# Keys and first queries of batch 0 turned by TensorE instead of DMA, and a first batch cut into more, smaller chunks

## The chip, the cores and the metric

The kernel runs on one core of a Trainium2 chip. The metric is the time of one execution on the device in microseconds (us). A core has TensorE (PE, with PEld for its weight loads), VectorE (DVE), ScalarE (ACT), GpSimd (POOL) and SyncE (SP), which in this kernel issues transfers; 16 DMA engines move data.

## The reference

Attention in which a query sees only keys of its own hash bucket, followed by a gated feed-forward layer. In short, with 4 batches, 8 heads, 768 tokens, a head size of 64 and 6 hash bits:

```python
q_bits = (np.einsum('bhsd,dk->bhsk', q, proj) > 0)          # keys alike; 6 bits make a bucket
mask   = q_bucket[:, :, :, None] == k_bucket[:, :, None, :]
scores = np.where(mask, scale * np.matmul(q, k.transpose(0, 1, 3, 2)), -1e9)
attn   = softmax(scores)                                    # over the keys
x      = np.matmul(attn, v)   -> (3072 tokens, 512)
out    = (x @ w_a) * (x @ w_b) @ w_out                      # 512 -> 1536 -> 512, all in float32
```

## The kernel before

Tokens are worked through in chunks. `BLOCKS` gives the length of each chunk in units of 128 tokens; the three later batches have three chunks of 256, batch 0 has chunks of 128, 128, 256 and 256. For each chunk the kernel does the attention of all 8 heads (units of one head and 128 queries) and then the feed-forward layer, `moe`. Chunks 0 and 1 (`N32`) do the layer in float32, while the weights' fp16 halves are not there yet; all later chunks use fp16 products, each float32 operand in a high and a low half.

**Keys and queries** go through `split` (L684), four pairs of heads of keys for a batch (`kprep`), queries once or twice per chunk (`qprep`). Its steps in batch 0: a bf16 product of the raw rows with themselves on PE (`gram`, L650) gives a bound, DVE reduces it (L637), and a power of two follows (`power_of`, L588 to L603); the high fp16 half is scaled (L621 on ACT, L623 on DVE), the low half is the rest (L717, DVE). High and low half, side by side in `kt0` or `qt0`, are turned (tokens from partitions to columns) by a transposing DMA that SP issues (L724) into half 1 of the buffer `trk` or `trq`. From that, PE makes the hash bits' products (L736, `kb` and `qb`), ACT copies the negated part (L754), DVE makes bits (L757) and penalty columns (L763, L766), which go beside a copy of the high half (L614) in `hp`; a second transposing DMA (L773) turns that into half 0. Only then can PE make scores (L1167).

**A unit**: scores, their maximum (`mx`, L1187, DVE), scale and bias (L1195, L1199), exponential (L1208, ACT). The exponentials are turned too: those of chunk 0 (`NTURN`) by PE in float32 (L1143, copies L614), the others by DMA after a split into fp16 halves. Then PE makes the weighted values `av` (L1221, L1236). When a chunk's units are done, `x` is scaled, turned, and the layer's products follow: first layer L1394 (float32) or L1402 (fp16), the gate `g` (L1431, DVE, with ACT's part L1423), second layer L1467.

**Weights** come as 128x1024 pieces (L886, issued by SP), and three operations make proper float32 out of each: two on ACT (L897, sometimes POOL at L899, and L907) and a join on DVE (L915). Six bf16 products (L933) bound them; later fp16 halves are made (L623, L858).

**The order** is not that of the code. Every operation goes through `op(engines, cost, run, key, r=..., w=...)`; `Plan.issue` starts them in a planned time, each engine in its own order, by the priorities of a table `PLACES` and on the engines that a table `ENGINES` names, where an operation allows several. On the chip each engine then runs its instructions in that fixed order and waits on semaphores for what an instruction needs. SP's queue of transfers is such an order too: a transfer that waits for its source holds up what stands behind it.

The step that the change replaces, in `split`, is this one, and a second of its kind for half 0:

```python
op(
    "SP", T_ISSUE,
    lambda: nc.sync.dma_start_transpose(out=dst.t[:, 1], in_=fl(pt[0])),
    key, r=[(pt[0], "hi"), (pt[0], "lo")], w=[(dst, 1)], svc=0.175 * n, hold=[dst],
)
```

Of the kernel before, what the change touches and what calls it, by code (L numbers as in the profile page):

```python
# [1568 lines left out]
```

## Time and profile before

| what | value |
|---|---|
| three timed runs | 914.08, 918.28, 919.96 us (median 918.28) |
| the profiled execution's own time | 915.97 us |
| its span (first to last instruction) | 914.2 us |
| PE busy | 867.5 us, 95% |
| DVE busy | 621.5 us, 68% |
| ACT busy | 569.5 us, 62% |
| POOL busy | 434.8 us, 48% |
| transfers of SP's queue | 147.44 MB, 82.9% of 16 DMA engines' span |

How to read what follows. A row of the table by stage has the stretch in us from the span's start, its length, then for PE, PEld, DVE, ACT and POOL the busy us and in brackets the number of instructions, then the granted clock of PE (1.00 is full speed), the DMA engines' busy share and GB/s. A row of the timeline has the start, the length, engine, line, operation, output<-inputs with shapes, the count, and in square brackets the idle time ahead of it and what ended it. A row of the lines has line, engine, operation, output<-inputs, shape and count, then busy us and mean ns of one, then idle time ahead of it and what ended it.

### The profile page before, as it was taken

To read this page: it belongs to the slowest core of one execution; us is meant where nothing else is said; L and a number is where in the kernel's file an instruction comes from. 1 tells how busy PE (TensorE), PEld (TensorE's weight loads), DVE (VectorE), ACT (ScalarE), POOL (GpSimd) and SP (SyncE) were. 2 spreads that over 40 slices of the span, in tenths; PEclk is the share of its full clock that TensorE was granted. 3 is DMA by queue.
4 is the path that set the end of the run, shared out by engine and by line. 5 is a ranking of instruction groups with operands and counts; after the bars stand their busy time and mean duration, and the time that the engine had idled before them with its cause. 6 is when DMAs were issued, how large, how long until landed. Compare 5 with 4: busy or idle time off the path is not lost. (4 is left out here: it accounts for less than half of the span.)

```text
span 914.2 us, 23474 instructions
## 1 busy us (share of the span) xinstructions
PE 867.5 (95%) x9361; PEld 662.7 (72%) x9361; DVE 621.5 (68%) x1441; ACT 569.5 (62%) x1126; POOL 434.8 (48%) x359
## 2 busy tenths in 40 slices
...
GB/s 303 253 323 290 274 123 123 160 145 180 193 191 195 158 157 140 136 182 200 199 185 115 158 158 143 161 192 158 196 186 124 118 162 118 131 121 105 36 1 24
DMA packets 444062, 148.94 MB, mean 163 GB/s; under 512 B 416688, under 2 KB 436272, under 8 KB 443952
## 3 DMA queue, kind: packets, MB, share of 16 engines
q1 hardware_dynamic: 443952, 147.44, 82.9%
q8 instruction: 73, 1.20, 0.5%
...
## 5 line engine op out<-in xcount | busy, mean ns | idle before, releaser
L617 POOL TENSOR_TENSOR a<-e,a 128x768 f16<-128x768 f32 x184 | 311.3, 1694 | 218.2 <-DVE a L614 90.1
L1402 PE MATMUL ab<-xT,wz 128*128 128x256 f16 x3168 | 374.5, 273 | 7.1 <-DVE g L1431 7.1
L1402 PEld LDWEIGHTS <-wz 128*128 128x128 f16 x3168 | 303.5, 98 | 55.8 <-issue 9.1
L1208 ACT ACTIVATE e<-s,bias,sc 128x768 f32<-128x768 f32 x192 | 189.5, 987 | 123.3 <-DVE bias L1199 116.0
L1187 DVE TENSOR_REDUCE mx<-s 128x1 f32<-128x768 f32 x192 | 182.4, 952 | 70.5 <-PE s L1167 69.7
L1467 PE MATMUL o<-wz,g 128*128 128x512 f16 (+1 forms) x840 | 216.2, 392 | 1.8 <-DVE g L1431 1.8
L1447 POOL TENSOR_TENSOR g<-g,g 128x256 f16<-128x256 f32 x132 | 92.2, 698 | 156.4 <-ACT g L1442 156.0
L1167 PE MATMUL s<-trk,trq 76*128 76x384 f16 (+1 forms) x768 | 155.3, 329 | 9.6 <-DMA trk<-hp 4.9
L1431 DVE SCALAR_TENSOR_TENSOR g<-ab,ab,a 128x256 f32<-128x256 f32 x132 | 63.5, 481 | 113.9 <-ACT a L1423 97.1
L1236 PEld LDWEIGHTS <-at 128*128 128x128 f16 x3312 | 117.1, 98 | 21.0 <-issue 3.5
L1467 PEld LDWEIGHTS <-g 128*128 128x128 f16 x792 | 75.0, 98 | 68.9 <-issue 0.6
L1236 PE MATMUL av<-vh,at 128*128 128x64 f16 x2208 | 121.0, 193 | 0.7 <-DMA at<-a 0.7
L1423 ACT ACTIVATE a<-ab,ab 128x256 f32<-128x256 f32 x132 | 62.2, 471 | 92.0 <-PE ab L1402 87.2
L1167 PEld LDWEIGHTS <-trq 76*128 76x128 f16 (+1 forms) x768 | 71.6, 99 | 56.5 <-issue 16.0
L614 ACT CAST a<-e 128x768 f16<-128x768 f32 x109 | 90.4, 829 | 1.8 <-DMA at<-a 0.2
L1442 ACT CAST g<-g 128x256 f16<-128x256 f32 x132 | 52.9, 401 | 41.2 <-DVE g L1431 39.3
L1236 PE MATMUL av<-vl,at 128*128 128x64 f16 x1104 | 62.5, 194 | 0.0
L614 DVE CAST a<-e 128x768 f16<-128x768 f32 x70 | 42.8, 614 | 21.4 <-ACT e L1208 20.9
L1394 PE MATMUL ab<-xT,wz 128*128 128x128 f32 x384 | 49.0, 279 | 1.6 <-DVE g L1431 1.6
L1394 PEld LDWEIGHTS ab<-xT,wz 128*128 128x128 f32 x384 | 46.1, 192 | 3.8 <-DVE g L1431 1.8
L1199 DVE TENSOR_SCALAR bias<-mx,sc 128x1 f32<-128x1 f32 x185 | 39.6, 214 | 6.5
L1195 DVE TENSOR_SCALAR sc<-mx,cq 128x1 f32<-128x1 f32 x185 | 39.2, 212 | 5.3
...
## 6 DMA issues: line engine op xcount, KB each, us to landing
...
at<-a SPq DMA_TRANSPOSE x184, 3.9
```

Source lines behind the costliest of these rows:

```text
L614: {"ACT": nc.scalar.copy, "DVE": nc.vector.tensor_copy, "POOL": nc.gpsimd.tensor_copy}[e](out=out, in_=x)
L617: (nc.gpsimd if e == "POOL" else nc.vector).tensor_tensor(out=out, in0=x, in1=y, op=ALU.subtract)
L1167: nc.tensor.matmul(ps.t[:, jj, :HALF], lhsT=trq.t[rows, i, (2 * j + h) * nt + t], rhs=tr.t[rows, i, k0 : k0 + NT // 2].rearrange("p n s -> ...
L1187: lambda: nc.vector.tensor_reduce(out=mx.t[:, col], in_=halves(ps.t), axis=AX.XY, op=ALU.max, negate=True),
L1208: lambda: nc.scalar.activation(flat2(e.t), halves(ps.t), AF.Exp, bias=bias.t[:, col], scale=sc.t[:, col], accum_out=sm.t[:, u : u + 1],),
L1236: nc.tensor.matmul(av.t[:, u, :], lhsT=at.t[:, a + kt, :], rhs=w.t[:, h, kt, :], start=i == 0, stop=i == 3 * NT - 1,)
L1394: nc.tensor.matmul(pl.t[:, m, to], lhsT=wt32(m, cc, f), rhs=xt.t[:, cc * nt // NC, cc * nt % NC : cc * nt % NC + nt, :], start=cc == 0, st ...
L1402: nc.tensor.matmul(pl.t[:, m, to], lhsT=wt(m, wi, cc, f), rhs=xt.t[:, cc * nt // NC, xi, cc * nt % NC : cc * nt % NC + nt, :], start=i == ...
L1423: lambda a=a, pl=pl, gr=gr, sc_of=sc_of: nc.scalar.activation(a.t, pl.t[:, 0, :CH], AF.Copy, scale=sc_of(gr)),
L1431: lambda a=a, g32=g32, pl=pl, gr=gr, sc_of=sc_of: nc.vector.scalar_tensor_tensor(out=g32.t, in0=pl.t[:, 1, :CH], scalar=sc_of(gr + 1), in1 ...
L1447: lambda g=g, g32=g32, g_of=g_of: nc.gpsimd.tensor_tensor(out=g_of(g[1]), in0=g32.t, in1=g_of(g[0]), op=ALU.subtract),
L1467: nc.tensor.matmul(po[u].t.rearrange("p a b -> p (a b)"), lhsT=x()[:, us], rhs=w, start=f == 0 and i == 0, stop=f == NF - 1 and i == len(t ...
```

## The change

In batch 0 the DMA turns of all four pairs of keys, and those of the first chunk's queries, become products on PE with an fp16 identity, into PSUM, each followed by a copy to `trk` or `trq`. Batch 0's chunks become 128, 128, 128, 128 and 256 tokens long, so that chunks 2 and 3, which use fp16 products in the layer, are 128 tokens long where one of 256 stood. Some of the planner's costs are changed, and both tables, `PLACES` and `ENGINES`, are new throughout.

```diff
-BLOCKS = ((1, 1, 2, 2), (2, 2, 2), (2, 2, 2), (2, 2, 2))
+BLOCKS = ((1, 1, 1, 1, 2), (2, 2, 2), (2, 2, 2), (2, 2, 2))
+K_PE, Q_PE = {0: (0, 1), 1: (0, 1), 2: (0, 1), 3: (0, 1)}, {0: (0, 1)}
...
+    identh = cp.tile([P, P], F16, tag="identh", name="identh")
+    op("DVE", 0.2, lambda: nc.vector.tensor_copy(out=identh, in_=ident), -85, r=["csb"], w=["identh"])
...
-    def split(raw, x, n, side, b, key, toks, tag, fast):
+    def split(raw, x, n, side, b, key, toks, tag, by_pe=()):
...
-        op(
-            "SP", T_ISSUE,
-            lambda: nc.sync.dma_start_transpose(out=dst.t[:, 1], in_=fl(pt[0])),
-            key, r=[(pt[0], "hi"), (pt[0], "lo")], w=[(dst, 1)], svc=0.175 * n, hold=[dst],
-        )
+        def turn(i, toks):
+            if i not in by_pe:
+                op(
+                    "SP", T_ISSUE,
+                    lambda: nc.sync.dma_start_transpose(out=dst.t[:, i], in_=fl(pt[1 - i])),
+                    key, r=toks, w=[(dst, i)], svc=0.175 * n, hold=[dst],
+                )
+                return
+            ps = psum(f"{which}t{i}_{x}")
+            flat = lambda: ps.t.rearrange("p a b -> p (a b)").bitcast(F16)[:, : n * P]
+
+            def tps():
+                for c in range(n):
+                    nc.tensor.transpose(
+                        out=flat()[:, c * P : (c + 1) * P], in_=fl(pt[1 - i])[:, c * P : (c + 1) * P],
+                        identity=identh,
+                    )
+
+            op("PE", 0.06 * n, tps, key, r=[*toks, "identh"], w=[ps])
+            op(
+                "ACT DVE", {"ACT": 0.22 + 0.83e-3 * n * P, "DVE": 0.2 + 1.04e-3 * n * P},
+                lambda e: cast(e, dst.t[:, i].rearrange("p n s -> p (n s)"), flat()), key, r=[ps], w=[(dst, i)],
+            )
+
+        turn(1, [(pt[0], "hi"), (pt[0], "lo")])
...
-        op("ACT", 0.26, lambda: nc.scalar.copy(out=six(neg), in_=cols(1)), key, r=[psb], w=[neg])
+        op("ACT", 0.2, lambda: nc.scalar.copy(out=six(neg), in_=cols(1)), key, r=[psb], w=[neg])
...
-        op(
-            "SP", T_ISSUE,
-            lambda: nc.sync.dma_start_transpose(out=dst.t[:, 0], in_=fl(pt[1])),
-            key, r=[(pt[1], "hi"), (pt[1], "hot")], w=[(dst, 0)], svc=0.175 * n,
-        )
+        turn(0, [(pt[1], "hi"), (pt[1], "hot")])
...
-        trk[b, hp], kinv[b, hp] = split(raw, f"{b}_{hp}", NK, 0, b, key, [raw], tag, b == 0)
+        trk[b, hp], kinv[b, hp] = split(raw, f"{b}_{hp}", NK, 0, b, key, [raw], tag, () if b else K_PE.get(hp, ()))
...
-        trqs[m, half], qinv[m, half] = split(raw, n, NQ, 1, b, key, [raw], tag, b == 0)
+        trqs[m, half], qinv[m, half] = split(raw, n, NQ, 1, b, key, [raw], tag, Q_PE.get(m, ()))
...
-            "ACT", 1.22,
+            "ACT", 1.14,
```

Of the tables, one line before and after:

```diff
-    162, 298, 731, 669, 323, 76, 57, 187, 50, 71, 1, 37, 438, 319, 258, 38, 453, 322, 119, 28, 439, 5, 145, 67, 378,
+    542, 57, 60, 78, 532, 427, 626, 28, 375, 268, 639, 631, 227, 105, 358, 88, 170, 1355, 1547, 35, 679, 95, 56,
```

What the new tables do is seen in the engines' orders. Two places follow. A name like `trk_0_1_320` is the buffer `trk` of batch 0, pair 1, with a running number.

The first is SP's queue at the program's start. Before, it reads from the first weight loads on:

```order
L886 DMA wz_70<-in_moe_w_a_dram 128x1024 x2
L1017 DMA v0_2_141<-in_v_dram 128x2x384
L724 DMA_TRANSPOSE trq_0_0_170<-qt0_0_0_139 128x8x128
L969 DMA rk_0_2_182<-in_k_dram 128x2x384
L724 DMA_TRANSPOSE trk_0_0_190<-kt0_0_0_160 128x12x128
L886 DMA wz_70<-in_moe_w_a_dram 128x1024
L969 DMA rk_0_3_208<-in_k_dram 128x2x384
L886 DMA wz_70<-in_moe_w_a_dram 128x1024
L773 DMA_TRANSPOSE trq_0_0_170<-hp0_75 128x8x128
L886 DMA wz_70<-in_moe_w_b_dram 128x1024
L773 DMA_TRANSPOSE trk_0_0_190<-hp1_76 128x12x128
L886 DMA wz_70<-in_moe_w_b_dram 128x1024
```

After, from the third weight load on; ahead of this piece stand the projection `pj`, the loads of all keys and values, the first queries, the identity and two weight loads:

```order
L920 DMA wz_70<-in_moe_w_a_dram 128x1024
L1130 DMA rq_1_0_289<-in_q_dram 128x8x64
L920 DMA wz_70<-in_moe_w_a_dram 128x1024
L920 DMA wz_70<-in_moe_w_b_dram 128x1024 x3
L1130 DMA rq_4_1_430<-in_q_dram 128x4x128
L920 DMA wz_70<-in_moe_w_b_dram 128x1024
L920 DMA wz_70<-in_moe_w_out_dram 128x1024 x2
L1130 DMA rq_2_0_488<-in_q_dram 128x8x64
L920 DMA wz_70<-in_moe_w_out_dram 128x1024 x2
L920 DMA wz_70<-in_moe_w_a_dram 128x1024
L1130 DMA rq_5_0_616<-in_q_dram 128x4x128
L744 DMA_TRANSPOSE trq_1_0_623<-qt0_1_0_561 128x8x128
```

The turns of keys and of the first queries are gone from the queue; the first transposing DMA left in it is that of chunk 1's queries, behind 13 weight loads. The projection moved from behind the loads of keys and values to the front.

The second place is ACT's first operations. Before:

```order
L621 ACTIVATE qt0_0_0_139<-rq_0_0_87,ai_q0_0_132 128x8x64
L614 COPY hp0_75<-qt0_0_0_139 128x8x64
L621 ACTIVATE kt0_0_0_160<-rk_0_0_91,ai_k0_0_153 128x12x64
L628 ACTIVATE pjx_66,st_pj_180<-pj_65 128x6
L897 ACTIVATE wz_70<-wz_70 128x1024
L907 ACTIVATE wz_70<-wz_70 128x1024
L621 ACTIVATE kt0_0_1_236<-rk_0_1_97,ai_k0_1_211 128x12x64
L754 COPY neg_q0_0_243<-qb_0_0_227 128x48
L621 ACTIVATE vh_0_1_258<-v0_1_93,v_ai_246 128x768
L621 ACTIVATE vh_0_0_264<-v0_0_99,v_ai_246 128x768
```

After:

```order
L632 COPY hp0_76<-kt0_0_0_154 128x12x64
L639 ACTIVATE qt0_0_0_184<-rq_0_0_94,ai_q0_0_173 128x8x64
L632 COPY trk_0_0_213<-kt1_0_0_189 128x1536
L632 COPY trq_0_0_238<-qt1_0_0_219 128x1024
L792 COPY neg_k0_0_261<-kb_0_0_240 128x72
L792 COPY neg_q0_0_292<-qb_0_0_263 128x48
L941 ACTIVATE wz_70<-wz_70 128x1024
L931 ACTIVATE wz_70<-wz_70 128x1024
L632 COPY trk_0_0_213<-kt0_0_0_297 128x1536
L639 ACTIVATE vh_0_3_368<-v0_3_135,v_ai_341 128x768
L792 COPY neg_k0_1_377<-kb_0_1_355 128x72
L632 COPY trq_0_0_238<-qt0_0_0_344 128x1024
```

The copies out of PSUM, `trk<-kt` and `trq<-qt` at L632, are new there; the two weight steps L941 and L931 (L907 and L897 before) stand ahead of the copy that fills the second half of the first keys; the scaling of the keys' high halves has gone from ACT.

## Rows read from the trace of the kernel before

**Rows 1.** The page's first part: busy us, share of the span, instructions by engine.

```profile
PE 867.5 (95%) x9361; PEld 662.7 (72%) x9361; DVE 621.5 (68%) x1441; ACT 569.5 (62%) x1126; POOL 434.8 (48%) x359
```

**Rows 2.** The table by stage, from first score to end of dense work.

```profile
0.00:27.00 27.00, 8.84 (x88) 6.66 (x89) 17.80 (x58) 13.26 (x18) 2.20 (x7) 1.00 1.02 294
27.00:143.20 116.20, 102.07 (x1003) 82.97 (x1003) 99.92 (x199) 82.75 (x133) 46.91 (x33) 0.96 1.01 243
143.20:186.00 42.80, 41.25 (x471) 32.07 (x470) 39.16 (x87) 28.42 (x50) 22.58 (x15) 1.00 0.92 156
186.00:905.00 719.00, 710.02 (x7775) 538.20 (x7776) 462.87 (x1096) 443.14 (x923) 361.69 (x302) 1.00 0.80 147
```

**Rows 3.** The timeline of PE, DVE and SP's queue (SPq), to the first scores.

```profile
4.80 1.20 SPq L557 DMA_DIRECT2D pj<-in_proj_dram  x2
...
5.80 0.82 PE L650 MATMUL gram_k<-rk 128*128 128x128 bf16 x6 [1.33 <-DMA rk<-in_k_dram]
...
9.79 1.64 DVE L717 SCALAR_TENSOR_TENSOR kt<-rk,ai_k,kt 128x768 f16<-128x768 f32 x1
...
11.85 2.87 SPq L724 DMA_TRANSPOSE trk<-kt  x1
...
18.01 0.47 PE L736 MATMUL kb<-pjw,trk 128*128 128x12 f16 x12
...
20.49 1.79 SPq L773 DMA_TRANSPOSE trk<-hp  x1
...
27.00 2.72 PE L1167 MATMUL s<-trk,trq 76*128 76x384 f16 x8 [3.67 <-DMA trk<-hp]
```

**Rows 4.** The table by stretch again, around the fall of PE's clock.

```profile
27.00:40.00 13.00, 10.12 (x97) 7.62 (x97) 10.48 (x34) 9.32 (x15) 0.00 (x0) 1.00 1.21 252
40.00:60.00 20.00, 18.06 (x137) 15.42 (x137) 14.35 (x35) 11.33 (x21) 2.30 (x2) 0.74 1.14 288
48.00:54.00 6.00, 6.00 (x29) 5.22 (x28) 4.45 (x12) 2.47 (x8) 1.03 (x1) 0.50 1.20 266
```

**Rows 5.** PE's narrow products: two of its timeline, three groups of its lines.

```profile
56.52 0.82 PE L1143 MATMUL et<-ident,e 128*128 128x128 f32 x6
...
68.28 1.08 PE L933 MATMUL gram_w<-wz 128*128 128x128 bf16 x16
...
L933 PE MATMUL gram_w<-wz 128*128 128x128 bf16 x96 | 7.5, 238 | 0.1
...
L650 PE MATMUL gram_k<-rk 128*128 128x128 bf16 x24 | 3.3, 305 | 3.7 <-DMA rk<-in_k_dram 3.7
...
L1402 PE MATMUL ab<-xT,wz 128*128 128x256 f16 x3168 | 374.5, 273 | 7.1 <-DVE g L1431 7.1
```

**Rows 6.** Copies by ACT and DVE, from the lines kept apart by shape.

```profile
L614 ACT COPY at<-et 128x384 f32<-128x384 f32 x9 | 4.2, 472 | 2.8 <-PE et L1143 2.5 <-PE ps_q L588 0.4
...
L614 ACT COPY xT<-px 128x512 f32<-128x512 f32 x2 | 1.1, 574 | 0.2 <-PE px L1328 0.2
...
L614 DVE COPY at<-et 128x384 f32<-128x384 f32 x7 | 3.8, 549 | 0.3 <-PE et L1143 0.3
...
L614 DVE COPY osb<-o 128x512 f32<-128x512 f32 x2 | 1.4, 685 | 0.7 <-PE o L1467 0.7
...
L614 DVE COPY hp<-kt 128x768 f16<-128x768 f16 x3 | 1.1, 351 | 0.6 <-ACT kt L621 0.6
```

**Rows 7.** ACT: its first weight step in the timeline, the value casts by line.

```profile
13.34 1.10 ACT L897 ACTIVATE wz<-wz 128x1024 int32<-128x1024 uint8 x1 [2.01 <-DMA wz<-in_moe_w_a_dram]
...
L621 ACT ACTIVATE vh<-v,v_ai 128x768 f16<-128x768 f32 x3 | 2.6, 925 | 0.7 <-DVE v_ai L603 0.7
```

**Rows 8.** DVE's waits of stage two (27 to 143.2): total us, times, longest.

```profile
DVE mx L1187 <- PE s L1167: 7.9, 9, 1.8
```

**Rows 9.** PE's timeline after chunk 1's layer: the long wait, and 256-column products.

```profile
185.88 1.99 PE L1467 MATMUL o<-wz,g 128*128 128x512 f32 x4 [1.15 <-DVE g L1431]
...
188.22 1.48 PE L1402 MATMUL ab<-xT,wz 128*128 128x256 f16 x12
```

More of the change, by code (lines that the diff above doesn't have):

```diff
@@ L61 @@
 PLACES = (
[192 rows of a table removed]
[193 rows of a table added]
 )
 ENGINES = {
-    16: "ACT", 19: "POOL", 30: "ACT", 33: "ACT DVE", 47: "ACT DVE", 58: "DVE", 61: "ACT", 95: "ACT", 106: "DVE",
-    109: "ACT", 115: "DVE", 118: "DVE", 120: "ACT", 125: "DVE", 130: "DVE", 139: "ACT", 144: "DVE", 147: "ACT",
-    163: "DVE", 172: "DVE", 175: "DVE", 183: "ACT", 189: "ACT", 192: "DVE", 203: "ACT", 209: "DVE", 211: "ACT DVE",
-    220: "ACT", 228: "DVE", 235: "DVE", 237: "ACT DVE", 243: "DVE", 245: "ACT", 252: "DVE", 262: "DVE", 270: "ACT",
-    278: "ACT", 287: "ACT", 292: "ACT", 301: "POOL", 313: "ACT", 318: "POOL", 327: "ACT", 332: "ACT", 346: "ACT",
@@ L261 @@
-    353: "ACT", 358: "ACT", 367: "POOL", 372: "ACT", 381: "POOL", 386: "ACT", 497: "DVE", 499: "ACT", 501: "DVE",
-    507: "ACT", 515: "ACT", 517: "DVE", 519: "ACT", 521: "ACT", 525: "ACT", 527: "ACT", 538: "DVE", 541: "ACT DVE",
-    552: "ACT POOL", 558: "DVE", 560: "ACT DVE", 566: "DVE", 568: "ACT POOL", 576: "ACT DVE", 583: "POOL",
-    585: "POOL", 599: "DVE", 601: "POOL", 607: "POOL", 609: "ACT POOL", 617: "ACT", 618: "POOL", 625: "DVE",
-    639: "ACT DVE", 655: "DVE", 661: "DVE", 663: "ACT POOL", 672: "DVE POOL", 678: "DVE", 680: "ACT DVE",
@@ L266 @@
-    686: "DVE", 688: "ACT POOL", 694: "DVE", 696: "POOL", 705: "DVE", 793: "DVE", 805: "ACT DVE", 814: "POOL",
-    816: "ACT", 822: "DVE", 830: "DVE", 832: "ACT DVE", 838: "DVE", 840: "DVE", 847: "DVE", 849: "POOL", 855: "DVE",
-    857: "ACT", 863: "DVE", 865: "ACT POOL", 873: "ACT POOL", 892: "DVE", 901: "DVE", 903: "ACT POOL", 909: "POOL",
-    917: "DVE", 919: "DVE", 925: "DVE", 927: "DVE", 934: "DVE", 936: "ACT DVE", 942: "DVE", 944: "ACT DVE",
-    950: "POOL", 952: "ACT DVE", 958: "DVE", 960: "ACT", 968: "ACT", 969: "DVE", 1059: "DVE", 1065: "ACT",
@@ L271 @@
-    1081: "ACT", 1091: "ACT", 1094: "ACT", 1104: "ACT", 1116: "DVE", 1122: "DVE", 1140: "ACT", 1165: "DVE",
-    1173: "DVE", 1181: "DVE", 1189: "ACT", 1198: "DVE", 1199: "POOL", 1218: "DVE", 1245: "DVE", 1253: "ACT",
-    1269: "DVE", 1278: "ACT", 1286: "DVE", 1422: "DVE", 1430: "DVE", 1455: "ACT", 1471: "DVE", 1479: "DVE",
-    1495: "DVE", 1498: "ACT", 1509: "ACT", 1675: "ACT", 1759: "DVE", 1806: "ACT", 2105: "DVE", 2182: "ACT",
-    2301: "DVE", 2546: "DVE", 2573: "ACT", 2606: "DVE", 2685: "ACT", 2976: "DVE", 3292: "DVE", 3436: "DVE",
@@ L276 @@
-    3515: "DVE",
+    17: "DVE", 21: "ACT DVE", 33: "DVE", 37: "ACT POOL", 43: "ACT", 52: "DVE", 53: "POOL", 59: "DVE", 68: "ACT",
+    69: "DVE POOL", 81: "ACT", 85: "DVE", 106: "DVE", 108: "DVE", 112: "ACT", 117: "POOL", 120: "ACT", 122: "ACT",
+    129: "ACT", 131: "ACT", 136: "DVE", 139: "ACT", 141: "ACT", 148: "ACT", 155: "POOL", 158: "ACT", 160: "DVE",
+    164: "DVE", 167: "DVE", 169: "DVE", 174: "POOL", 177: "ACT", 179: "ACT", 183: "POOL", 188: "DVE", 194: "DVE",
+    200: "ACT", 203: "ACT POOL", 214: "DVE", 222: "DVE POOL", 231: "ACT POOL", 237: "POOL", 239: "DVE POOL",
@@ new lines @@
+    246: "POOL", 254: "POOL", 256: "DVE POOL", 263: "DVE", 265: "ACT", 271: "DVE", 273: "POOL", 281: "ACT",
+    284: "ACT", 289: "ACT", 329: "ACT", 338: "ACT", 352: "POOL", 357: "POOL", 364: "POOL", 369: "POOL", 383: "ACT",
+    397: "POOL", 500: "ACT", 508: "ACT", 510: "ACT", 512: "ACT", 516: "ACT", 518: "ACT", 520: "DVE", 526: "DVE",
+    532: "ACT", 538: "ACT", 542: "ACT", 549: "DVE", 552: "ACT DVE", 561: "DVE", 563: "DVE", 571: "ACT DVE",
+    578: "DVE", 588: "ACT POOL", 595: "DVE", 597: "ACT POOL", 614: "POOL", 622: "ACT DVE", 630: "DVE", 631: "POOL",
@@ new lines @@
+    695: "DVE", 716: "ACT", 722: "DVE", 724: "DVE POOL", 741: "POOL", 750: "ACT DVE", 756: "DVE", 758: "ACT DVE",
+    765: "DVE", 767: "ACT", 773: "DVE", 775: "POOL", 784: "DVE", 848: "ACT", 855: "ACT", 858: "POOL", 869: "DVE",
+    875: "POOL", 883: "DVE", 891: "DVE", 893: "DVE POOL", 902: "ACT", 910: "ACT DVE", 926: "ACT DVE", 935: "POOL",
+    942: "DVE", 945: "ACT DVE", 954: "DVE", 956: "ACT DVE", 962: "DVE", 964: "ACT", 970: "POOL", 972: "ACT DVE",
+    978: "DVE", 980: "ACT", 987: "DVE", 989: "ACT", 995: "DVE", 997: "DVE POOL", 1003: "DVE", 1005: "ACT DVE",
@@ new lines @@
+    1011: "DVE", 1021: "ACT", 1110: "ACT", 1112: "DVE", 1121: "DVE", 1131: "ACT", 1134: "ACT", 1144: "ACT",
+    1163: "DVE", 1169: "ACT", 1175: "DVE", 1193: "DVE", 1209: "DVE", 1218: "DVE", 1226: "ACT", 1234: "ACT",
+    1251: "ACT", 1271: "ACT", 1274: "DVE", 1284: "DVE", 1298: "ACT", 1322: "DVE", 1339: "ACT", 1347: "ACT",
+    1453: "DVE", 1455: "DVE", 1461: "ACT", 1483: "ACT", 1491: "ACT", 1499: "ACT", 1516: "DVE", 1524: "DVE",
+    1541: "DVE", 1548: "ACT", 1551: "ACT", 1570: "DVE", 1578: "ACT", 1586: "ACT", 1595: "ACT", 1603: "DVE",
@@ new lines @@
+    1619: "DVE", 1629: "DVE", 1717: "ACT", 1719: "ACT", 1725: "ACT", 1739: "ACT", 1747: "ACT", 1763: "DVE",
+    1780: "ACT", 1788: "DVE", 1796: "ACT", 1812: "ACT", 1815: "ACT", 1826: "ACT", 1842: "ACT", 1859: "ACT",
+    1867: "ACT", 1883: "ACT", 1981: "ACT", 1983: "ACT", 1992: "DVE", 2005: "DVE", 2018: "ACT", 2046: "DVE",
+    2064: "DVE", 2080: "DVE", 2097: "ACT", 2105: "DVE", 2113: "DVE", 2123: "POOL", 2169: "ACT", 2177: "DVE",
+    2185: "DVE", 2193: "ACT", 2202: "DVE", 2210: "ACT", 2236: "POOL", 2326: "ACT", 2332: "DVE", 2335: "ACT",
@@ new lines @@
+    2346: "DVE", 2354: "DVE", 2370: "ACT", 2387: "ACT", 2395: "ACT", 2413: "POOL", 2422: "ACT", 2441: "DVE",
+    2449: "DVE", 2482: "ACT", 2499: "ACT", 2588: "ACT", 2590: "DVE", 2618: "DVE", 2634: "ACT", 2659: "DVE",
+    2667: "ACT", 2676: "ACT", 2677: "POOL", 2697: "DVE", 2705: "DVE", 2713: "ACT", 2721: "DVE", 2730: "ACT",
+    2738: "DVE", 2754: "ACT", 2763: "ACT", 2852: "DVE", 2854: "ACT", 2860: "DVE", 2873: "ACT", 2905: "ACT",
+    2911: "ACT", 2917: "ACT", 2927: "ACT", 2951: "ACT", 2968: "DVE", 2976: "ACT", 2984: "ACT", 3000: "ACT",
@@ new lines @@
+    3003: "ACT", 3013: "DVE", 3026: "DVE", 3048: "ACT", 3064: "ACT", 3089: "ACT", 3097: "DVE", 3106: "DVE",
+    3195: "ACT", 3197: "ACT", 3203: "ACT", 3206: "ACT", 3225: "ACT", 3233: "DVE", 3241: "ACT", 3266: "ACT",
+    3274: "ACT", 3283: "ACT", 3320: "ACT", 3328: "DVE", 3345: "DVE", 3470: "ACT", 3489: "DVE", 3497: "DVE",
+    3505: "DVE", 3514: "ACT", 3538: "DVE", 3554: "ACT", 3568: "DVE", 3576: "ACT", 3584: "DVE", 3601: "ACT",
+    3609: "ACT", 3617: "DVE", 3625: "DVE", 3634: "DVE", 3635: "DVE", 3723: "DVE", 3725: "ACT",
```

8 lines of the change are left out of this document (4 added, 4 removed), and 383 rows, old and new, of the table PLACES.

## The prediction

> **What bounds the kernel now.** I read the page first: TensorE (PE) is busy for 867.5 of 914.2 us, the others for far less [rows 1]. So the first question is where PE's 46.7 idle us lie, and the table by stage answers it [rows 2]. It is cut at four instants: the first score product (27.0), the first second-layer product of chunk 1 (143.2), that chunk's last one (186), the end of the last long stretch of dense work (905). Idle are 27.0 - 8.8 = 18.2, 116.2 - 102.1 = 14.1, 42.8 - 41.3 = 1.5 and 719 - 710 = 9.0; the remaining 3.9 lie in the tail. In the 719 us the work is the same before and after the change and PE is 98.8% busy: a new order can win 9 us there at most. All else is in the first 143 us.
>
> Stage one is a chain, not a load: DVE is busy for 17.8 of its 27 us, ACT for 13.3. The rows of the first pair of keys show it [rows 3]. The bound is taken at 5.80, the low half of the keys is ready at 9.79 + 1.64 = 11.43, the DMA turn is issued at 11.85 and PE can use its result at 18.01, 6.2 us on; the second turn is issued at 20.49 and the first scores start at 27.00, 6.5 us on, after PE stood idle for 3.67 us on that landing. So 12.7 of 27 us pass between an issue of a turn and the use of it.
>
> Stage two has DVE at 99.9 of 116.2 us: it sets the pace, with 16.3 us idle. About a third of that, 5.7 us, lies between 40 and 60 us, where PE's granted clock was at 0.50 from 48 to 54, the lower of its two levels (1.2 of 2.4 GHz); before, from 27 to 40, PE had worked 10.1 of 13 us [rows 4].
>
> **The change, part by part.**
>
> *Turns on PE.* Ten DMA turns leave SP: eight of keys, two of queries. PE gets 8 x 12 + 2 x 8 = 112 products of 128 columns. The nearest rows are 128-column products in bf16 with weights of their own: sixteen in 1.08 us late, (1.08 - 0.24)/15 = 0.056 us each, but six in 0.82 early, (0.82 - 0.305)/5 = 0.103 us each [rows 3, 5]. So 112 cost 6.3 us (all late) to 11.6 us (all early). 52 of them stand ahead of the first score: 5.4 us at the early price, inside 18.2 us of idle time, and so free. The other 60 cost 3.4 us at the late price, in a stage in which PE waits for DVE: nothing, while PE's 14.1 idle us there cover it; 3.4 to 6.2 if they are gone.
>
> *The copies.* Each PE turn lands in PSUM and must be copied: ten copies, seven by ACT, three by DVE. No row has 1536 columns. ACT took 0.472 us for 384 columns out of PSUM and 0.574 for 512, so 0.8 ns a column: 1.39 us for 1536, 0.98 for 1024. DVE took 0.549 and 0.685: 1.06 ns a column, 1.77 us for 1536 [rows 6]. ACT: 5 x 1.39 + 2 x 0.98 = 8.9 us; DVE: 3 x 1.77 = 5.3 us. (As fp16 out of SBUF, 768 columns took DVE 0.351; that is the lower end, 2.1 us in all.)
>
> *First score.* The keys' load is now issued behind the two small ones of the projection, which hold SP for 1.20 us [rows 3], where the queries' load ahead of it held it for 0.5, so all of it moves by 0.7: low half at 12.1. PE's turn 12 x 0.103 + 0.2 = 1.4, copy 1.4, bits on PE 0.5, ACT and DVE steps on them 0.8, second turn 1.4, copy 1.4: 6.9 us where the two DMA turns and the steps between took 15.6 (11.43 to 27.00). But ACT is in order. Ahead of the second copy it now has the queries' copy (1.0) and two weight steps (1.1 each) that start only when their load has landed, and behind it one value cast (0.93) and the queries' second copy (1.0), which the score needs too [rows 7]. That is 5.1 us more: 12.1 + 6.9 + 5.1 = 24.1. Ends: 19 (nothing in the way) and 29 (the load that ACT waits for lands 5 us late; its first weight step waited 2.01 before). I take 24: **-3.0**.
>
> *Stage two.* SP's queue, where weight loads stood behind turns that waited for their source, now issues 13 weight loads ahead of its first turn, where it issued 2; so weights are loaded and joined earlier (17 instead of 12 joins ahead of the first second-layer product of chunk 0), and values' low halves (4 x 1.01) move behind the first score. To the same point, the second-layer product of chunk 1, DVE's order counts: maxima 28 to 24 (-3.8 us), scale and bias pairs 24 to 14, ten of them to POOL (-4.3), value lows +4 (+4.0), key copies +2 (+3.5), weight joins +1 (+1.4), fp16 lows of weights +1 (+1.5) and highs -2 (-2.2), copies of turned exponentials -3 (-1.6), the weights' common bounds +2.0: **+0.5 us of DVE work, as good as none**. So DVE's load does not shrink here; what can shrink is its 16.3 us of idling. Queued DMA turns no longer stand between a pair of keys and its scores, and of DVE's idle time 7.9 us were waits for scores [rows 8]. I take away 5, about the idle time of 40 to 60 us: **-5.0**. Ends: -13, for PE has 103 us of work there, and +6, if the four key copies behind the first score (2 x 1.77 on DVE, 2 x 1.39 on ACT) find no idle time at all.
>
> By PE's order, chunk 1's second layer then starts with 2.2 us less of the unchanged work done (fewer scores, fp16 products). That is left for later: **+2.2**. In exchange DVE, by the counts of its order times its durations, has 28 instead of 37 us in the next stage, where PE's waits were 1.5, 1.15 of it one wait for g [rows 9]: **-1.0**.
>
> *Two chunks of 128 instead of one of 256.* 576 products of 128 columns take the place of 288 of 256. 256 columns: twelve in 1.48 us, one of them 0.273, so (1.48 - 0.273)/11 = 0.110 us each [rows 5, 9]; 128: 0.056 by the late row [rows 5]. 576 x 0.056 - 288 x 0.110 = **+0.8** with rounding. Lower end 0. The upper end is the early price: 576 x 0.103 - 288 x 0.110 = +28; I take the row of the sixteen, for these too stand late, in dense work, each with weights of its own. The Trainium skill ("TensorE: Matmul & The Clock Gate", Back-to-back issue gap) has a sustained pair of load and product at about 81 ns for 128 columns, which speaks against this change; estimated by it, the halves would add 15 us. The trace does not agree: the sixteen pairs ran at 56 ns.
>
> Planner costs (exponential 1.22 to 1.14 and the like) change nothing that runs; they go with the new table of places.
>
> *Sum* against the profiled run's 915.97 us: -3.0 - 5.0 + 2.2 - 1.0 + 0.8 = -6.0, 910 us. The three timed runs have a median 2.3 us above that run; I add half of it: **911 us**.
>
> **Rivals.**
>
> *Stage two runs at PE's pace.* If ACT and DVE interleave well enough, DVE's idle time of 16.3 goes nearly whole and the stage ends at -13 instead of -5: 903. With a first score at 21 it is 900. For it: POOL takes ten scale pairs, PE's clock may not fall this time. Against it: ACT's work up to the same place doesn't fall either.
>
> *The DMA turns were hidden.* Stage one is then held by the loads of the last keys and values, which are still 8 x 384 KB, and stage two by DVE as before: only +0.8 and +2.2 are left, 919. For it: DMA is as busy as ever in both stages (share 1.02 and 1.01 [rows 2]). Against it: the 3.67 us wait on a turn's landing [rows 3].
>
> *Copies in the way (slower).* Place: ACT, ahead of the first score. If the weight step that it must run before the second key copy waits past 27 us less the 3.3 us that follow it, the lead is gone; at its late end the score comes at 29 (+2.0), and the four later copies cost their 6.3: 915.97 + 2.0 + 6.3 + 2.2 + 0.8 = 927. It decides from a weight load that lands after about 21 us. A later time still, 937, comes if the 576 narrow products run at the early price (910 - 0.8 + 27.6).
>
> *Turns that leave PE's clock low.* PE ran at the lower level from 48 to 54 us [rows 4]. If the 60 turns behind the first score run at 0.103 each and the products near them too, PE loses 60 x 0.047 = 2.8 us on them and about as much again on the products: 911 + 5.6 = 917. Against: six turns, in fp32, took 0.82 us at 56.52, no more than the early products [rows 5]. The Trainium skill (same page, Part 4: PE-mode transpose) has about 275 ns for a turn in a kernel and says that turns do not count as work that lifts the clock; estimated by it, the 60 would cost 16.5 us. The trace does not agree on the price, with six in 0.82; whether turns alone lift the clock no row shows.
>
> **How the numbers follow.** Forecast 0.50, with a range of its own of 906 to 916; stage two at PE's pace 0.27 (898 to 906); hidden or clock-bound 0.16 (916 to 921); slower 0.07 (921 to 937, the narrow products' +28 with it). 8 in 10: 901 to 921. About 1% is what a measurement of this kernel tells from no change. Of 918.28 that is below 909.1 or above 927.5: faster 0.27 + 0.11 (the lower part of the forecast) = 0.38; slower 0.05; same 0.57.
>
> **What would show it.** First score at 24 (right between 22 and 26); no DMA wait ahead of it; copies near 1.4 and 1.8 us; 128-column products at 0.056; the first second-layer product of chunk 1 near 135 (143.2 - 3 - 5); PE at 98 to 99% from there to the end. It is wrong if ACT waits for a weight load in front of a key copy, if PE's clock is at 0.5 for over 10 us, or if the later 700 us, which I leave as they were, lose or gain more than 4.

## The result and the profile after

The changed kernel takes 907.68 us (median of 4 runs, 906.16 to 908.83) where the kernel before took 917.58 (median of 4, 914.08 to 919.96): a ratio of 0.9894, 95% interval 0.9857 to 0.9931, 9.9 us less. The profiled execution took 906.16 us with a span of 904.4, against 915.97 and 914.2.

The page's first part after the change, to be held against [rows 1]:

```profile
PE 869.7 (96%) x9761; PEld 672.7 (74%) x9761; DVE 621.4 (69%) x1434; ACT 578.5 (64%) x1135; POOL 449.2 (50%) x378
```

PE is busy for 2.2 us more and the span is 9.8 us shorter, so 12 us of PE's idle time are gone: 914.2 - 867.5 = 46.7 before, 904.4 - 869.7 = 34.7 after. The table by stage of the changed kernel, cut at the same events as [rows 2] (first score at 22.18, first second-layer product of chunk 1 at 133.67, the end of that chunk's last one at 177.56):

```profile
0.00:22.18 22.18, 11.35 (x150) 9.96 (x150) 14.05 (x55) 11.23 (x16) 2.20 (x7) 1.00 0.89 301
22.18:133.67 111.49, 99.72 (x1001) 84.53 (x1001) 99.28 (x197) 83.36 (x128) 52.23 (x49) 0.94 0.86 222
133.67:177.56 43.89, 43.89 (x502) 34.47 (x502) 36.86 (x70) 27.72 (x50) 23.34 (x17) 1.00 0.70 127
177.56:895.20 717.64, 710.06 (x8090) 541.55 (x8089) 469.94 (x1112) 454.58 (x942) 370.21 (x305) 1.00 0.83 150
```

[Rows 2] cut at the start of chunk 1's last second-layer product; with the cut at its end the same two stages of the kernel before are:

```profile
143.17:187.87 44.70, 43.15 (x480) 32.92 (x479) 40.99 (x90) 30.32 (x52) 23.13 (x17) 1.00 0.92 157
187.87:905.00 717.13, 708.15 (x7771) 537.38 (x7768) 461.07 (x1093) 441.27 (x921) 361.13 (x300) 1.00 0.80 147
```

Stage by stage: the first score 27.00 to 22.18, -4.8; stage two 116.17 to 111.49, -4.7; stage three 44.70 to 43.89, -0.8; the long stage 717.13 to 717.64, +0.5; the tail 9.2 both times. So nearly all of the gain lies ahead of chunk 1's second layer. The cut at the first score shares it out by place and not by cause: chunk 0's second layer begins at 86.66 before and at 86.94 after, and by then DVE has been busy for 73.5 us instead of 64.6. The new order does more of DVE's work early.

The timeline of the first pair of keys, DVE, PE and ACT of the changed kernel, is to be held against [rows 3]:

```profile
5.58 0.82 PE L668 MATMUL gram_k<-rk 128*128 128x128 bf16 x6 [0.38 <-DMA rk<-in_k_dram]
...
7.91 0.62 DVE L641 TENSOR_SCALAR kt<-rk,ai_k 128x768 f16<-128x768 f32 x1
8.56 1.02 DVE L735 SCALAR_TENSOR_TENSOR kt<-rk,ai_k,kt 128x768 f16<-128x768 f32 x1
...
11.67 0.23 DVE L578 CAST identh<-ident 128x128 f16<-128x128 f32 x1 [0.79 <-DMA ident<-in_cst_dram]
...
12.14 1.48 PE L753 MATMUL kt<-identh,kt 128*128 128x128 f16 x12
...
13.65 1.44 ACT L632 COPY trk<-kt 128x1536 f16<-128x1536 f16 x1 [2.03 <-PE kt L753]
...
15.15 0.49 PE L774 MATMUL kb<-pjw,trk 128*128 128x12 f16 x12
...
16.76 1.16 ACT L941 ACTIVATE wz<-wz 128x1024 f32<-128x1024 f32 x1
...
17.36 0.83 PE L753 MATMUL kt<-identh,hp 128*128 128x128 f16 x12
...
18.83 1.45 ACT L632 COPY trk<-kt 128x1536 f16<-128x1536 f16 x1
...
21.08 1.04 ACT L632 COPY trq<-qt 128x1024 f16<-128x1024 f16 x1
...
22.18 1.15 PE L1201 MATMUL s<-trk,trq 76*128 76x384 f16 x4 [2.42 <-ACT trq L632]
```

From the first turn's product to the bits' product 15.15 - 12.14 = 3.0 us pass where 6.2 passed from issue to use before; from the second turn's product to the end of its copy 20.28 - 17.36 = 2.9. What ends PE's wait ahead of the first score is now ACT's copy of the queries, not a DMA.

Copies and narrow products, from the lines kept apart by shape:

```profile
L632 ACT COPY trk<-kt 128x1536 f16<-128x1536 f16 x5 | 7.2, 1442 | 2.0 <-PE kt L753 2.0
...
L632 DVE COPY trk<-kt 128x1536 f16<-128x1536 f16 x3 | 2.8, 948 | 0.0
L632 ACT COPY trq<-qt 128x1024 f16<-128x1024 f16 x2 | 2.1, 1026 | 0.1
...
L1436 PE MATMUL ab<-xT,wz 128*128 128x128 f16 x576 | 37.1, 219 | 0.0
```

In stage two, DVE waits less than half as long for scores as in [rows 8]:

```profile
DVE mx L1221 <- PE s L1201: 3.8, 7, 1.0
```

### The profile page after: what moved, and what is told of

It reads as the page before. It is cut to its first block, busy times and chain, and to the rows that moved or that the text cites. A ratio compares the mean times of both kernels' runs of the same rounds, so it can differ in the third digit from the quotient of the medians.

```text
span 904.4 us, 24308 instructions
## 1 busy us (share of the span) xinstructions
PE 869.7 (96%) x9761; PEld 672.7 (74%) x9761; DVE 621.4 (69%) x1434; ACT 578.5 (64%) x1135; POOL 449.2 (50%) x378
## 4 chain that ended last, share of the span: by engine, by line
PE 78%; DMA 8%; DVE 7%; issue 3%; ACT 2%; POOL 1%; SPq 1%; DVEq 0%; ACTq 0%; POOLq 0%
PE ab L1436 34%; PE o L1501 18%; PE s L1201 11%; PE av L1270 9%; PE ab L1428 3%; DMA at<-a 2%; DMA wz<-in_moe_w_out_dram 1%; DMA wz<-in_moe_w_a_dram 1%; DVE mx L1221 1%; DMA rq<-in_q_dram 1%; DVE wz L892 1%; DMA wz<-in_moe_w_b_dram 1%; DMA v<-in_v_dram 1%; DVE wz L949 1%; POOL a L635 1%
## 5 line engine op out<-in xcount | busy, mean ns | idle before, releaser
L1436 PE MATMUL ab<-xT,wz 128*128 128x256 f16 (+1 forms) x3456 | 377.8, 264 | 0.9 <-DVE g L1465 0.9
L1436 PEld LDWEIGHTS <-wz 128*128 128x128 f16 x3456 | 309.4, 98 | 46.9 <-issue 1.7
L632 ACT CAST a<-e 128x768 f16<-128x768 f32 x111 | 91.9, 828 | 2.8 <-DMA at<-a 0.3
L632 DVE CAST a<-e 128x768 f16<-128x768 f32 x66 | 40.2, 609 | 16.7 <-ACT e L1242 14.8
```

Of the source, the lines that this page charges most:

```text
L632: {"ACT": nc.scalar.copy, "DVE": nc.vector.tensor_copy, "POOL": nc.gpsimd.tensor_copy}[e](out=out, in_=x)
L1436: nc.tensor.matmul(pl.t[:, m, to], lhsT=wt(m, wi, cc, f), rhs=xt.t[:, cc * nt // NC, xi, cc * nt % NC : cc * nt % NC + nt, :], start=i == ...
```

## The experiments

All are timed in rounds beside the kernel before. The differences to the changed kernel below are those of the medians (907.68 us); the median of the kernel before lay between 915.98 and 917.58 in the five groups of runs, so a difference under 2 us says nothing. Set against the kernel before in the same rounds, every one of them comes out 0.5 to 1.6 us higher than in the table (dve_minus at -2.8 instead of -4.4).

| run | median us | ratio to before (95%) | us against the changed kernel |
|---|---|---|---|
| dma_turns | 925.03 | 1.0097 (1.0063 to 1.0131) | +17.3 |
| first_dma | 914.00 | 0.9975 (0.9959 to 0.9990) | +6.3 |
| late_dma | 916.99 | 1.0010 (0.9991 to 1.0030) | +9.3 |
| before_pe | 927.46 | 1.0137 (1.0094 to 1.0179) | (+11.4 against before) |
| before_pe2 | 924.72 | 1.0098 (1.0069 to 1.0127) | (+8.0 against before) |
| dve_plus | 919.53 | 1.0026 (1.0002 to 1.0050) | +11.9 |
| dve_minus | 903.32 | 0.9864 (0.9845 to 0.9884) | -4.4 |
| pe_plus | 910.56 | 0.9935 (0.9912 to 0.9958) | +2.9 |
| act_plus | 911.34 | 0.9934 (0.9913 to 0.9956) | +3.7 |
| pool_scale | 911.35 | 0.9929 (0.9902 to 0.9955) | +3.7 |
| steps_late | 908.27 | 0.9903 (0.9868 to 0.9938) | +0.6 |
| halves2 | 914.63 | 0.9980 (0.9964 to 0.9997) | +7.0 |

### Are the turns the cause, or the new order?

For the first five runs and two later ones the planner's choice is written out: a table `SEQ` of operation numbers and engines, in the order in which the planner of the changed kernel (or of the kernel before) started them, so that every engine keeps that order exactly. Then only the turns differ:

```diff
-K_PE, Q_PE = {0: (0, 1), 1: (0, 1), 2: (0, 1), 3: (0, 1)}, {0: (0, 1)}
+K_PE, Q_PE = {}, {}                                                # dma_turns
+K_PE, Q_PE = {1: (0, 1), 2: (0, 1), 3: (0, 1)}, {}                 # first_dma
+K_PE, Q_PE = {0: (0, 1)}, {0: (0, 1)}                              # late_dma
```

> The changed kernel with all ten turns by DMA again, every engine's other instructions in the changed kernel's own order (products and copies of the turns left out). Theory A (the latency of the turns is what was taken away): two turns stand ahead of the first score, each 6.3 us by DMA against 1.48 + 1.44 by product and copy, so the first score moves from 22.2 to 22.2 + 2 x 3.4 = 29; three later pairs of keys lose part of as much; total 915 to 922. Theory B (the new order and the smaller chunks brought the gain, the turns themselves were hidden): within 2 us of 907.7.

> The changed kernel with only the four turns by DMA that the first score needs (first pair of keys, first queries), the other six on TensorE, same order. Theory A: first score at 29, total 4 to 7 us more, 912 to 915. Theory C (DVE's load to chunk 0's layer sets the pace, since that layer's second products begin at 86.7 us before and at 86.9 after the change, so a lead at the first score is used up by then): total 0 to 2 us more. Theory B: no more than 2 as well, and the first score by 27.

> The changed kernel with the six turns of the later three pairs of keys by DMA, the first four on TensorE, same order. Theory A: first score as in the changed kernel, 22.2; scores of the later pairs late by 3 to 7 us each, partly beside other work; total 4 to 8 us more. Theory B: within 2 us of 907.7. If A holds for both, this and the run with the first four add up to the run with all ten, within 2 us.

Waits of PE in dma_turns, up to 150 us (columns: engine, output and line, what it waited for; us in all, times, longest):

```profile
PE kb L659 <- DMA trk<-kt: 11.8, 4, 5.1
PE s L1086 <- DMA trq<-hp: 6.6, 1, 6.6
```

One row each of ACT's and DVE's timeline in dma_turns:

```profile
52.12 0.62 ACT L515 COPY hp<-qt 128x512 f16<-128x512 f16 x1 [5.03 <-DMA trk<-hp]
55.19 2.36 DVE L834 SCALAR_TENSOR_TENSOR wz<-wz 128x1024 int32<-128x1024 int32 x2 [6.18 <-ACT wz L826]
```

The first scores with only the first four by DMA (PE's timeline), and PE's wait with only the later six by DMA:

```profile
27.81 1.46 PE L1086 MATMUL s<-trk,trq 76*128 76x384 f16 x4 [5.08 <-DMA trq<-hp]
```

```profile
PE kb L659 <- DMA trk<-kt: 7.6, 3, 4.1
```

The time is 17.3, 6.3 and 9.3 us longer; 6.3 + 9.3 = 15.6 lies within 2 of 17.3, as theory A asked. With ten the first score comes at 30.47, with four at 27.81 (5.6 us later), with the later six at 22.52. Theory B, that the turns were hidden, falls: PE waits for landings that were put back, and so does ACT, which stands 5.03 us for a turn that reads `hp`, with weight steps behind it on which DVE then waits 6.18. C falls too in this direction: in first_dma chunk 0's second layer begins at 96.00 instead of 86.94, and 6.3 us are left at the end. The 5.6 us at the first score were not simply carried through, for the delay is 9.1 us at that place. The losses are above A's numbers for dma_turns and late_dma (922 and 916 at most). A caveat is in the build: an order made for quick turns has each turn's use close behind it, so it is the worst host for slow ones, and what an order planned for DMA turns with these chunks would take was not tried. Nor do the runs part a turn's landing time from what it holds up in SP's queue, and none has the new order with the old chunks: what the smaller chunks are worth in the 9.9 us stays open.

The other direction puts the ten products and copies into the kernel before, in its own order and chunks, at the places where the DMA turns were issued:

> The kernel before with the same ten turns as products with an fp16 identity and copies (alternately ACT and DVE, at the place where the DMA turn was issued), and nothing else changed: its own chunks, its own order. Theory A: first score from 27.0 to about 20.5, total 911 to 914. Theory B: total 916 to 919, as before. A first score before 22 with an unchanged total speaks for C: what DVE has to do up to chunk 0's layer sets the pace.

It became slower, 927.46 us. DVE's timeline shows one reason, which was mine: I had put the identity's cast at the program's start.

```profile
10.60 0.23 DVE L461 CAST identh<-ident 128x128 f16<-128x128 f32 x1 [5.75 <-DMA ident<-in_cst_dram]
```

DVE stood for 5.75 us on a load that SP issues at 3.91, behind six others, with the bounds of the first keys behind that cast. The next run puts the cast beside the bf16 one:

```diff
-    op("DVE", 0.2, lambda: nc.vector.tensor_copy(out=identb, in_=ident), ...)
+    op("DVE", 0.2, lambda: [nc.vector.tensor_copy(out=x, in_=ident) for x in (identh, identb)], ...)
```

> As the run before_pe, but the identity's fp16 cast stands on DVE beside the bf16 cast, not at the program's start, where DVE waited 5.8 us for the identity to land (in that run's waits of DVE), and the first turn of the queries follows it. Theory A (latency alone decides): first score near 20.5 to 22, total 911 to 914. Theory O (on engines that run in order, products and copies put where the DMA turns were issued hold up what stands behind them, so the gain needs the new order): the first score moves from 33.7 by the 5.8 us to 28 and the total from 927.5 to about 921, still not below before.

The first score moved to 31.29 (28 was expected by theory O), the total to 924.72, still 8.0 us above the kernel before in the same rounds (916.68). PE's timeline shows why quicker turns alone do not help:

```profile
13.00 1.44 PE L634 MATMUL kt<-identh,kt 128*128 128x128 f16 x12
...
20.28 0.16 PE L487 MATMUL ps_k<-st_k,onesr 128*128 128x1 bf16 x1 [1.46 <-DVE st_k L536]
...
21.36 0.51 PE L656 MATMUL kb<-pjw,trk 128*128 128x12 f16 x12
...
29.65 1.44 PE L634 MATMUL kt<-identh,kt 128*128 128x128 f16 x12
...
31.29 2.72 PE L1086 MATMUL s<-trk,trq 76*128 76x384 f16 x8 [0.19 <-ACT trk L513]
```

The first keys are turned at 13.00, but the bits' product that needs them runs at 21.36: in the old order a bound of values, a bound of keys and the queries' second turn stand ahead of it on PE, and among them PE waits for DVE four times, 3.8 us in all. And the turns of the second and third pair, at 28.30 and 29.65, now stand ahead of the first scores on PE, where a DMA turn had its own queue. So A as I wrote it (latency alone decides) falls, O stands: quicker turns bring the gain, and of the two orders tried only the new one lets them, in which their products' users come soon and their neighbours do not block them. Turns and order cannot be shared out as two shares of 9.9 us, since either alone, as built here, is a loss.

### What sets the pace of stage two?

Work was added to one engine at a time in chunks 0 and 1, with the order unchanged, and once taken away:

```diff
 # dve_plus: each maximum twice            # act_plus: each exponential twice (same loop)
+            lambda: [nc.vector.tensor_reduce(...) for _ in range(2 if m < 2 else 1)],
 # pe_plus: each score product twice
-            for i in range(2):
+            for i in [0, 1] * (2 if m < 2 else 1):
 # dve_minus: the maximum over the first 384 of 768 keys
-                out=mx.t[:, col], in_=halves(ps.t), axis=AX.XY, op=ALU.max, negate=True
+                out=mx.t[:, col], in_=halves(ps.t)[:, : 1 if m < 2 else 2], axis=AX.XY, op=ALU.max, negate=True
```

> The changed kernel with each maximum over scores of chunks 0 and 1 taken twice on DVE (16 more of 0.95 us, 15.2 us), order unchanged. Theory D (DVE sets the pace of stage two, busy 99.3 of 111.5 us there): 8 to 15 us more, 916 to 923, the first second-layer product of chunk 1 from 133.7 to 142 to 149. Theory P (stage two runs at PE's pace or on chains through ACT): at most 4 us more.

> The changed kernel with the score products of chunks 0 and 1 made twice (64 more products of 384 columns; four took 1.15 to 1.44 us at the low clock and take about 0.65 at the full one, so 10.4 us or more of PE time in stage two), order unchanged. Theory D: PE's 11.8 idle us there cover most of it, 1 to 5 us more, 909 to 913. Theory P: 8 to 12 us more. If the fuller stretch from 22 to 38 us lifts PE's granted clock (0.53 and 0.65 there), part of it comes back.

> The changed kernel with each exponential of chunks 0 and 1 taken twice on ACT (16 more of 0.99 us and a 0.19 us read of the sum: 18.9 us), order unchanged. Theory D: ACT's 28 idle us in stage two (83.4 busy of 111.5) cover most: 2 to 6 us more. Theory L (the way of a unit from scores to exponential sets the pace): 10 to 18 us more.

> The changed kernel with the maxima of chunks 0 and 1 taken over the first 384 of 768 keys only (the second half is left out of the 16 maxima), order unchanged: each falls from 0.95 to about 0.5 us, 7.2 us off DVE. Theory D (DVE's load sets the pace of stage two; 15.2 us added cost 11.9, so 0.78 each): 4 to 6 us less, 902 to 904. Theory E (other bounds lie close behind, as PE's added 10.4 us cost about 3 and ACT's 18.9 cost 3.7): 0 to 3 us less.

The maxima over half the keys, from DVE's lines of dve_minus:

```profile
L1221 DVE TENSOR_REDUCE mx<-s 128x1 f32<-128x384 f32 x16 | 8.7, 551 | 3.6 <-PE s L1201 3.6
```

The rows with chunk 1's first second-layer product (133.67 in the changed kernel) in PE's timeline of dve_plus, pe_plus, act_plus and dve_minus:

```profile
144.69 1.88 PE L1504 MATMUL o<-wz,g 128*128 128x512 f32 x4
```

```profile
139.17 1.88 PE L1501 MATMUL o<-wz,g 128*128 128x512 f32 x4
```

```profile
140.98 1.88 PE L1504 MATMUL o<-wz,g 128*128 128x512 f32 x4
```

```profile
130.15 1.88 PE L1501 MATMUL o<-wz,g 128*128 128x512 f32 x4
```

Per us added, at the end: DVE 11.9 / 15.2 = 0.78, PE 2.9 / 10.4 = 0.28, ACT 3.7 / 18.9 = 0.20. Per us taken from DVE (16 maxima at 0.551 instead of 0.951, 6.4 us): 4.4 / 6.4 = 0.7, or 2.8 / 6.4 = 0.4 against the kernel before in the same rounds, so this run does not tell D's 4 to 6 us from E's 0 to 3. For added work theory D holds: DVE sets the pace of this stage more than any other engine. It is no pure bound, since at chunk 1's second layer DVE's extra work shows with 11.0 us of 15.2, PE's with 5.5 of 10.4 and ACT's with 7.3 of 18.9, part of which the later stages give back. Part of these prices may also be the clock's, and no run parts it off: from 40 to 60 us PE's granted clock read 0.74 in dve_plus, 0.83 in pe_plus and 0.73 in act_plus, where the changed kernel has 1.00.

That suggests taking real work off DVE. The two ways tried did not win:

```diff
 # pool_scale: the 14 scale and bias pairs that DVE has in stage two go to POOL (ten are there already)
-    ... 136D ... 145D ... 164D ... 212D ... 271D ...
+    ... 136G ... 145G ... 164G ... 212G ... 271G ...
 # steps_late: ACT's order around the queries' second copy (91); 285, 284 are the weight steps, 112 a value cast; DVE's join of that weight moves too
-    ... 87A,285A, ... 284A, ... 27A, ... 112A, ... 39A,91A, ...
+    ... 87A, ... 27A, ... 39A,91A,112A,285A,284A, ...
```

> The changed kernel with the 14 scale and bias pairs that DVE has before chunk 1's second layer moved to POOL (the other ten are there already), order unchanged. DVE loses 14 x 0.42 = 5.9 us; each pair takes 0.75 + 0.40 = 1.15 us on POOL instead of 0.42, so the way from scores to exponential is 0.7 us longer, 14 times. Theory D (DVE's load sets the pace; 15.2 us of added maxima cost 11.9, so 0.78 each): 4 to 5 us less, 903 to 904. Theory L (the way of a unit from scores to exponential sets it, since scores hold one of two PSUM buffers until the exponential): 1 to 6 us more.

The waits of ACT in stage two, of pool_scale (22 to 140 us) and then of the changed kernel (22 to 134):

```profile
ACT e L1125 <- POOL bias L1116: 20.7, 11, 3.3
```

```profile
ACT e L1242 <- DVE bias L1233: 11.7, 8, 4.2
```

5.9 us less on DVE became 3.7 us more at the end: ACT's exponentials wait 20.7 us for POOL's pairs instead of 11.7 for DVE's. So theory L has its part: these pairs lie on the way of a unit, and on POOL, where they take longer, they cost more than DVE's relief brought.

> The changed kernel with ACT's two weight steps and one value cast, which stand ahead of the copies that the first score needs, moved behind the last of these, and DVE's join of that weight behind the bound of the fourth pair of keys. Theory E (a lead at the first score reaches the end: 5.6 us later there cost 6.3 in the run first_dma): first score from 22.2 to 20.0 to 20.8, total 1 to 2 us less, about 906. Rival: the join and the weight steps late by 4 us hold DVE's queue and the next weight load, so the lead is gone by chunk 0's layer: 0 to 2 us more.

The first two units' scores in PE's timeline of steps_late:

```profile
20.07 0.83 PE L1084 MATMUL s<-trk,trq 76*128 76x384 f16 x4 [1.18 <-ACT trq L515]
...
33.64 1.18 PE L1084 MATMUL s<-trk,trq 76*128 76x384 f16 x4 [1.82 <-ACT e L1125]
```

The first score came 2.1 us earlier than the changed kernel's 22.18, the second unit's 1.0 later (32.61 in the changed kernel), and the total did not move. The lead is smaller than it looks: in six other runs with the changed kernel's instructions up to there the first score lay between 20.68 and 22.21. A delay at the first score was passed on (first_dma), this lead was not: it was gone by the second unit. That it is ACT's and DVE's unchanged work ahead of that unit which used it up is argued from their orders, not shown.

### What does a 128-column product cost?

```diff
-                        for wi, xi in ((0, 0), (1, 0), (0, 1)):
-                            for cc in range(NC):
-                                nc.tensor.matmul(pl.t[:, m, to], lhsT=wt(m, wi, cc, f), rhs=..., ...)
+                        for y in range(nt):                      # each half of 128 columns by itself
+                            for i in range(3 * NC):
+                                nc.tensor.matmul(pl.t[:, m, c : c + P], lhsT=wt(m, wi, cc, f), rhs=..., ...)
```

> The changed kernel with all 2880 first-layer products of 256 columns split into 5760 of 128, each with its own weights. By my price of 0.056 us against 0.110: 322.6 - 316.8 = 6 us more, 914. By the busy time per product that the changed kernel's lines show (37.1 us for 576, 340.7 for 2880): 371 - 341 = 30 us more, 938. If each waits for its weight load of 98 ns: 564 - 341 = 223 us more.

The long stage, cut at the same events as in the changed kernel, and the lines of PE in halves2 (products, then their weight loads):

```profile
176.69:901.90 725.21, 718.66 (x10965) 583.24 (x10963) 471.02 (x1112) 454.46 (x942) 369.99 (x305) 1.00 0.84 149
```

```profile
L1439 PE MATMUL ab<-xT,wz 128*128 128x128 f16 x6336 | 385.7, 219 | 1.1 <-DVE g L1467 1.0
L1439 PEld LDWEIGHTS <-wz 128*128 128x128 f16 x6336 | 364.1, 98 | 18.3 <-issue 2.2
```

Ten times the change's number of narrow products cost 7.0 us at the end and 725.2 - 717.6 = 7.6 in the stage, close to what the price of 0.056 us said (6). The busy time by product, which said 30, was no price here. The Trainium skill ("TensorE: Matmul & The Clock Gate", Back-to-back issue gap) gives about 81 ns for a sustained pair of weight load and 128-column product; estimated by it, these 5760 would have added some 150 us. The runs do not agree: with 0.110 us for a product of 256 columns, the 7.6 us make (2880 x 0.110 + 7.6) / 5760 = 0.056 us, 56 ns a pair.

## Why the prediction was right, step by step

It said 911 us, 901 to 921; measured were 907.68. Its steps:

**First score** (24.1 said, 22.18 measured, so -4.8 instead of -3.0; by the 20.68 to 22.21 of the runs above, -4.8 to -6.3). The prices on PE and ACT held but for one: turn 1.48 (1.4 said), copies 1.44 and 1.45 (1.4), second turn 0.83 (1.4). Two waits were other than said. The low half was ready at 9.58 instead of 12.1: the bound is taken at 5.58, where 6.5 was said (5.80 + 0.7), DVE also made the high half (0.62) and its low half took 1.02, not the 1.64 of [rows 3]; but the first turn had to wait until 12.14, because three bounds stand ahead of it on PE and the identity was cast only at 11.67, which the prediction had overlooked. And ACT, for which 5.1 us were charged, cost about half: the second turn's product ended at 18.19, its copy at 20.28 and the queries' at 22.12, against 19.6 had the copy followed at once. That ACT would wait for a weight load did not come true: the step at 16.76 follows without a wait.

**Stage two** (-5.0 said, -4.7 measured). The size was right, and the way to it is shown in part. DVE's load didn't shrink (99.89 to 99.28 us; +0.5 was said), its idle time did: 116.17 - 99.89 = 16.3 to 111.49 - 99.28 = 12.2. That its waits for scores fell by the same 4.1 us, 7.9 to 3.8, is partly luck: in halves2, which has the same instructions here and needs 111.96 us, they come to 4.9. dma_turns shows that queued turns, put into the new order, lengthen this stage to 121.89 us (30.47 to 152.36) with DVE busy for 98.30; but DVE's waits for scores are 5.0 there, and the longer ones lie behind ACT (6.2 for a weight step, 3.1 for bits). So the turns cost DVE idle time, as said; that they do it through the wait for scores is not shown. dve_plus shows that DVE sets the pace. One price inside was wrong and small: a DVE copy of 1536 columns took 0.948 us, not 1.77. I had it from float32 rows of [rows 6]; the other end of that group, fp16 within SBUF, was the nearer one. The Trainium skill ("VectorE: DVE Perf Modes", Why PSUM operands drop a tier) says that a 16-bit operand in PSUM may still go at twice the rate of float32, which would have told it. The trace agrees: half of the 1.06 ns a column of [rows 6], with the 0.14 us that those rows leave as a fixed part, gives an estimate of 0.96 us for 1536 columns.

**The rest** (+2.2 - 1.0 + 0.8 = +2.0 said; -0.8 + 0.5 = -0.3 measured). This is the mis-sized term. The work was sized well: PE's busy time in the two late stages rose from 43.15 + 708.15 to 43.89 + 710.06, 2.65 us, where 2.2 of deferred work and 0.8 for halves were said. PE's waits were not: they fell by 1.55 to nothing in stage three (1.0 said), and from 9.0 to 7.6 in the long stage, which I left as it was. There PE's waits before (to 905 us) and after the change (to 895) are of different kinds:

```profile
PE ab L1402 <- DVE g L1431: 7.1, 10, 1.2
```

```profile
PE av L1270 <- DMA at<-a: 3.0, 5, 1.1
PE s L1201 <- DVE bits_q L795: 2.3, 1, 2.3
PE s L1201 <- DVE po_t_v L618: 1.3, 1, 1.3
PE ab L1436 <- DVE g L1465: 0.9, 3, 0.3
```

The new order took away the first layer's waits for the gate and put smaller ones elsewhere. I had bounded that gain at 9 us and then counted none of it. All terms together were -6.0 us, and the two profiled runs differ by 9.8: the rest accounts for 2.3 of the 3.8 us missing, the first score for 1.8, and stage two was 0.3 too much.

**The rivals.** *Turns hidden* falls by dma_turns. *Stage two at PE's pace* falls by pe_plus (10.4 us added, 5.5 at chunk 1's second layer, 2.9 at the end). *Copies in the way* did not come up: no weight load held ACT ahead of the keys. *Clock left low* is the instructive one, for its sign did appear, and by the prediction's own last paragraph (0.5 for over 10 us) the forecast should have failed. The table by stretch of the changed kernel:

```profile
22.00:28.00 6.00, 3.71 (x31) 3.19 (x32) 5.14 (x13) 5.31 (x7) 3.26 (x3) 0.54 0.80 263
28.00:34.00 6.00, 5.43 (x54) 4.70 (x53) 5.51 (x15) 5.60 (x8) 2.21 (x3) 0.50 0.80 257
34.00:40.00 6.00, 5.41 (x63) 5.09 (x62) 5.04 (x11) 4.98 (x8) 1.55 (x3) 0.82 1.05 298
```

PE's granted clock is at its lower level (1.2 of 2.4 GHz) from soon after 22 to beyond 34, after an idle wait of 2.42 us ahead of the first score. Yet DVE and ACT are busy for 10.7 and 10.9 of these first 12 us: PE is slow where others set the pace, and the price put on it (5.6 us) was for a stretch in which PE does. A run made for another question bears this out. halves2 has the same instructions up to here, and its clock is low for a much shorter time:

```profile
22.00:28.00 6.00, 2.66 (x37) 2.66 (x35) 5.39 (x10) 5.32 (x5) 4.34 (x3) 0.85 0.83 272
28.00:34.00 6.00, 4.76 (x68) 4.15 (x67) 5.36 (x15) 5.61 (x8) 1.29 (x3) 0.86 1.00 324
```

Its first score came 1.3 us earlier (20.85), chunk 1's second layer 0.9 earlier (132.81): the faster clock added nothing to that lead. With one profile of each, the low clock cost about nothing here. The row that the prediction set against this rival, six turns in 0.82 us at 56.52, does not bear on it: from 54 to 60 us the clock read 1.00, and at 48.36, with the clock at 0.50, three such turns took 0.84.
